# P times v in one piece and w_v split during the second batch, in a fused attention, channel-mix and FFT kernel

## The chip, the cores and the metric

The kernel runs on one core of a Trainium2 chip, in one launch. The core has TensorE (matmul; its weight loads are a row of their own in the profile), VectorE, ScalarE, GpSimd, and the queue of SyncE (SP), which issues most transfers. The metric is the device time in microseconds, the median of several runs; lower is better.

## The reference, cut to what matters

```python
def attention(q, k, v, tau):          # 4 batches, 8 heads, 576 positions, head size 64
    s = q @ k.T / 8
    s = where(s >= s.max(-1) - tau, s, -1e9)
    p = exp(s - s.max(-1)); p /= p.sum(-1) + 1e-9
    return p @ v                       # "P times v"
def channel_mix(x, mu_k, mu_r, w_k, w_v, w_r):     # 512 -> 1024 -> 512
    xp = x shifted by one position
    xk = mu_k*x + (1-mu_k)*xp;  xr = mu_r*x + (1-mu_r)*xp
    return sigmoid(xr @ w_r) * (relu(xk @ w_k)**2 @ w_v)
def last(x, w_ch1, w_ch2):             # 512 -> 2048 -> 512
    u = x + real(fft2(x))
    return u + relu(layernorm(u) @ w_ch1) @ w_ch2
```

The output is last(channel_mix(attention(...))), in fp32.

## The kernel before, in words

Work is written as a Python program whose instructions a planner then orders: it simulates the engines and, for each engine, takes the ready instruction of the highest priority; priority is the order of the program, moved forward by the offset of the high_priority context around it. The table P holds these offsets and the pace of the parts. On the chip each engine works off its list in order.

Attention goes by head pairs: 4 batches x 4 pairs = 16 pairs, each of 9 steps (a step is one 128x576 score tile). ORDER has eight steps of one head (j = 0 or 1) with 128 queries (i = 0 to 3), and in the middle, as step 4, the mixed tile: the 2 x 64 remaining queries of both heads (name em). A step is: scores on TensorE (L218, L232), maximum, threshold and select on VectorE (L258, L273), exponential on ScalarE (L269), scaling by 1/sum on GpSimd (emit_norm, L279). Two steps later (LT) the tile is transposed (emit_T, L318, L326): 512 keys in four 128x128 transposes, and the remainder keys (512 to 575) of both heads in a fifth; ScalarE copies them out to pt (unit) and ptr (rem_unit). The mixed tile was transposed by emit_Tmix, called once for each half of the queries, as its rows belong to both: four transposes (L338) and two matmuls of the remainder keys against 64 rows and 32 columns (L349). P times v is emit_av: for a pair and a half (288 queries), five key blocks x two heads, the heads in the two halves of one PSUM bank, 64 columns of v each as weights (L372; the bank is called avs in batch one and av later). There are 32 such units. They are written by do_av at the steps AC = 7 and 10 after the pair's first.

The first batch (pi < NPAIR) runs attention alone. Beside it all_weights brings w_k (8 pieces of 512 columns), w_r (4) and w_v (7 of 8): a load on SP's queue, three VectorE operations that build fp32 from the raw words (L67 to L69), a copy to a high part (ScalarE, L72) and the subtraction for the low part (GpSimd, L73), in a pool stage1 with two raw buffers; WR pieces are written per step. From step 38 on stage1 is closed, the feed-forward pool (ffn) takes its place, and ffn_stream is drawn on by credits: CN per step, CA at steps with P times v. It computes for each half of a batch w_k (name kps, L392 to L394), w_r (rps, the same lines), w_v (vps, L504 to L506), and the transposes back (xn). The tile t of the gate shares its buffer with the raw words of the eighth piece of w_v, the generator state['late'], whose one load and split run in that pool with one buffer each; the stream finishes it before it writes the gate's matmuls. Pairs of later batches also load raw q and k through one buffer (rawqk, L154) and split them. When attention is over, the rest of the stream runs with the FFT, and then the last part (c1ps, c2ps, L951 to L966).

Of the kernel before, what the change touches and what calls it, by code (L numbers as in the profile page):

```python
# [9 lines left out]
F32 = mybir.dt.float32  # L10
F32R = mybir.dt.float32r
I32 = mybir.dt.int32
ALU = mybir.AluOpType
AF = mybir.ActivationFunctionType
# [4 lines left out]
B, H, S, DH = 4, 8, 576, 64  # L19
D, FF, FC = 512, 1024, 2048  # L20
HS = S // 2
NPAIR = H // 2
P = dict(PRI=100, SR=1.0, CR=2, ORD=0, PF=0, CB=0, XT=0, XL=0, K2=0, FE=0, FE3=0, MU=0, WP=256, C1=2, RB=4, BB=2, FT=4, A0=[7, 8], A1=[11, 12], B0=[7, 8], B1=[11, 12], PT4=1, OR0='', XH=0, SP0=0, CA=1.48, CN=2.22, QS=1, pF=100, pM=100, pN=100, pT=100, pO=100, pE=100, pS=100, pA=0, pX=0, NA=0, LT=2, WS=3, WR=1, CC=3.0, BN=2, OR='FATXOESBI', TM=8, SO=0, SO0=0, AO=0, AO0=0, QS0=0, XD=0, TH=0, SM=0, SM0=0, N0=34, qF=100, qM=100, qN=100, qT=100, qO=100, qE=100, qS=100, qA=100, qX=30, RQ=[0,0,0,0,0,0,0,0], XN=0, QN=36, AVR=0, LX=2, WD=0, WP2=512, E3=1, NA0=0, W0=0, XD2=0, PO=0, WP1=512, IN=[0,1,2,2,4,5,6,7])
P.update({'AC': (7, 10), 'CA': 0.5, 'CN': 2.1, 'pX': 100, 'CR': 3, 'pA': 100, 'OR': 'FTBXOAESI', 'PF': 300, 'pE': 0, 'pO': 500, 'QS': 2, 'WS': 0, 'FE3': 2, 'pF': 0, 'A0': [7, 10], 'C1': 3, 'BN': 2, 'K2': 0, 'WR': 0.6, 'FT': 2, 'MU': 0, 'SR': 0.6, 'XT': 0, 'SO0': 239, 'XL': 3, 'QS0': 2, 'FE': 2, 'CB': 2, 'AO0': 8, 'IN': [0, 0, 2, 2, 5, 6, 6], 'pN': 30, 'pM': 0, 'A1': [10, 13], 'AVR': 1, 'NA0': 170, 'N0': 30, 'PT4': 0, 'WD': 1, 'qN': 0, 'qS': 500, 'qT': 150, 'QN': 37, 'qE': 0, 'qO': 30, 'B0': [7, 10], 'qX': 60, 'qM': 500, 'E3': 1, 'WP1': 512, 'qF': 300, 'OR0': 'FTBXEOASI', 'B1': [10, 13], 'TH': 4, 'AO': 4, 'qA': 30, 'pS': 300, 'SO': 16, 'RQ': [0, 0, 0, 0, 0, 0, 0, 0]})
PRI = P['PRI']


# [1 line left out]
def tile_kernel(ctx: ExitStack, tc: tile.TileContext, a):  # L29
    nc = tc.nc  # L30
    pe, dve, act, pool, sp = nc.tensor, nc.vector, nc.scalar, nc.gpsimd, nc.sync
# [3 lines left out]
    pst = ctx.enter_context(tc.tile_pool(name="pst", bufs=2, space=PSUM))  # L35
# [4 lines left out]
    ident = const.tile([128, 128], F32, name="ident")  # L40
# [37 lines left out]
    def whole(pair, base=0):  # L78
        return lambda c, n: [x[:, c - base:c - base + n] for x in pair]
# [9 lines left out]
    wk = [big(f"A{i}", f"wk{i}") for i in range(2)]  # L89
    wv = [big(f"B{i}", f"wv{i}") for i in range(2)]  # L90
    wr = [wC.tile([128, 2048], F32R, name=f"wr{i}") for i in range(2)]
# [3 lines left out]
    at = astack.enter_context(tc.tile_pool(name="at", bufs=1, side="right"))  # L95
# [40 lines left out]
    NPI = B * NPAIR  # L136
# [100 lines left out]
    def eview(n):  # L237
        pi, tl = step_of(n)
        if tl is None:
            if n not in em:  # L240
                em[n] = at.tile([128, S], F32, tag="em", name="em")
            return em[n]
        j, i = tl
        if (pi, i) not in et:
            m = 4 * pi + i
            if P['E3'] and m % 3 == 2 and m < 4 * NPAIR - 2:
                et[pi, i] = stage.tile([128, 2 * S], F32, tag="e", name="e3")
            else:
                et[pi, i] = at.tile([128, 2 * S], F32, tag="e", bufs=2, name="e")
        return et[pi, i][:, j * S:(j + 1) * S]  # L250
# [25 lines left out]

    def emit_norm(n):
        st, e = stat[n], eview(n)
        pool.tensor_scalar(e, e, st[:, 2:3], 1.0, op0=ALU.mult, op1=ALU.mult)  # L279

    def emit_front(n):
# [14 lines left out]
    def unit(pi, half):  # L296
        if (pi, half) not in ptu:
            ptu[pi, half] = at.tile([128, 2, 4, HS], F32, tag="pt", bufs=3, name="pt")
        return ptu[pi, half]

    def rem_unit(pi, half):
        if (pi, half) not in ptr:
            ptr[pi, half] = at.tile([128, HS], F32, tag="ptr", bufs=2, name="ptr")
        return ptr[pi, half]

    def emit_T(n):
        if not 0 <= n < NSTEP:
            return []
        pi, tl = step_of(n)
        if tl is None:  # L310
            return emit_Tmix(pi, 0)
        j, i = tl
        e = et[pi, i]
        o = 640 if j else 0
        half, sl = i // 2, slice(128 * (i % 2), 128 * (i % 2) + 128)
        t = pst.tile([128, 4, 128], F32, tag="t", name="t")
        for k in range(4):
            pe.transpose(t[:, k, :], e[:, o + 128 * k:o + 128 * (k + 1)], ident)  # L318

        def out():  # L320
            act.activation(unit(pi, half)[:, j, :, sl], t, AF.Copy)  # L321

        todo = [out]
        if j == 1:
            t2 = pst.tile([128, 128], F32, tag="t", name="t2")
            pe.transpose(t2, e[:, 512:640], ident)  # L326

            def out2():
                act.activation(rem_unit(pi, half)[:, sl], t2, AF.Copy)

            todo.append(out2)
        return todo

    def emit_Tmix(pi, half):
        e = em[pi * 9 + 4]
        t = pst.tile([128, 4, 2, 2, 32], F32, tag="t", name="tm")
        for k in range(4):
            pe.transpose(t[:, k].rearrange("p a b c -> p (a b c)"), e[:, 128 * k:128 * (k + 1)], ident)  # L338
        sl = slice(256, HS)

        def out():
            for j in range(2):
                act.activation(unit(pi, half)[:, j, :, sl], t[:, :, j, half, :], AF.Copy)

        def out2():
            t2 = pst.tile([128, 32], F32, tag="t", name="tm2")
            for j in range(2):
                c = 64 * j + 32 * half
                pe.matmul(t2[64 * j:64 * j + 64], e[:, 512:576], ident[:, c:c + 32], start=True, stop=True)  # L349
            act.activation(rem_unit(pi, half)[:, sl], t2, AF.Copy)  # L350

        return [out, out2]

# [11 lines left out]
    def emit_av(pi, half):  # L365

        ps = bank([128, HS], "av")
        v, u, r = vts[pi], ptu[pi, half], ptr[pi, half]
        for k in range(5):
            for j in range(2):  # L370
                w, x = (v[:, 4 * j + k, :], u[:, j, k, :]) if k < 4 else (v[:, 8 + j, :], r)
                pe.matmul(ps[64 * j:64 * j + 64], w, x, start=(k == 0), stop=(k == 4))  # L372

        def post():
            b, pr = divmod(pi, NPAIR)
            x = xunit(pi, half)
            act.activation(x[:, 1:], ps, AF.Copy)
            if half == 1:
                dve.tensor_copy(x[:, 0:1], xT[b, pr, 0][:, HS:HS + 1])
            xdone[half] += 1  # L380

        pending.append(post)


    ffn = {}
# [175 lines left out]
    sstack = ExitStack()  # L561
    stage = sstack.enter_context(tc.tile_pool(name="stage1", bufs=1, side="left"))

    late = 4096 - P['WD'] * P['WP2']

    def all_weights():
        for src, w in (("w_k", wk), ("w_r", wr), ("w_v", wv)):
            yield from weight_pieces(a[src], whole(w), stage, P['WP1'], 0, late if src == "w_v" else None)

    wgen = all_weights()  # L570
    for _ in range(P['W0']):
# [62 lines left out]
    def do_out(n, pi, s):  # L634
        with hp('pO'):
            for f in outs_of.pop(n):
                f()
        do_mix(n, pi, s)

    def do_mix(n, pi, s):  # L640
        if s == P['TM'] and 0 <= pi + (s < 7) * -1 < NPI:
            with hp('pO'):
                for f in emit_Tmix(pi + (s < 7) * -1, 1):
                    f()

    def do_exp(n, pi, s):
        with hp('pE'):
# [12 lines left out]
    def do_X(n, pi, s):  # L660
        if pi < NPAIR:
            if n >= P['WS']:
                state['w'] += P['WR']
                while state['w'] >= 1:
                    state['w'] -= 1
                    next(wgen, None)
        elif state['stream'] is None:
            if n < 9 * NPAIR + 2:
                return
            for _ in wgen:  # L670
                pass
            sstack.close()
            ffn["pool"] = fstackp.enter_context(tc.tile_pool(name="ffn", bufs=1, side="left"))
            state['stream'] = ffn_stream()
            state['late'] = weight_pieces(a["w_v"], whole(wv), ffn["pool"], P['WP2'], late, None, 1, 1, ("t", "xn"))
        elif n < NSTEP:
            with hp('pX'):
                state['credit'] = min(state['credit'] + (P['CA'] if any(s + x in P['AC'] for x in (0, 9)) else P['CN']), P['CC'])
                while state['credit'] > 0:
                    got = next(state['stream'])  # L680
                    if not got:
                        break
                    state['credit'] -= got
                next(state['late'], None)
# [12 lines left out]
    for n in range(NSTEP + 8):  # L697
        pi, s = divmod(n, 9)
# [491 lines left out]
```

## Time and profile before

| | |
|---|---|
| time, median of 3 runs | 1146.96 us (1145.16 to 1150.7) |
| the profiled execution | 1144.78 us, its span 1143.0 us |
| granted TensorE clock, mean | 0.978 |
| busy, share of the span | TensorE 94%, VectorE 60%, ScalarE 45%, GpSimd 36% |

The profile is of one execution. Its time is the device time that the runs report too; the span is from its first to its last instruction. Matmuls are pipelined and their ends are modelled, so the starts of successive matmuls tell more than their durations. av, kps and so on are names of tiles; "x2" in a row is two records.

### The profile page before, as it was taken

Reading aid. Unit: us, or ns where it says so; the run is one execution under the profiler, and the core shown is the slowest. Engines: PE = TensorE matmul, PEld = TensorE weight load, DVE = VectorE, ACT = ScalarE, POOL = GpSimd, SP = SyncE. Lnnn points to the kernel's source line nnn. Section 1 sums busy time; section 2 is a strip of 40 time slices with the busy share of each in tenths; the row PEclk is TensorE's granted clock in tenths of the full one; section 3 lists DMA queues with packets and bytes.
Section 4 is the critical chain, followed back from the end, with each engine's and each line's share of the span. In section 5 each row is a group of like instructions: output and inputs, shape, how many; then the busy total and the mean of one; then the engine's idle time right before and its main releaser. Section 6 shows DMA issues by size and latency. Waiting matters only on the chain.

```text
span 1143.0 us, 19326 instructions
## 1 busy us (share of the span) xinstructions
PE 1072.7 (94%) x7109; PEld 920.4 (81%) x7109; DVE 680.7 (60%) x1765; ACT 519.7 (45%) x1243; POOL 411.9 (36%) x552
## 2 busy tenths in 40 slices
PE   5988689999989989989999987999999999999998
PEld 4655577787877877878789977888989999999997
DVE  6888885555564575576535678975643859323222
ACT  4766666474574674674726644423322222111111
POOL 2434576254363454463523254520010636100000
PEclk9999899999999989999999978999999999999999
DMA  6433311101111120120053245653432546223231
GB/s 234 136 111 116 108 52 49 56 23 55 56 52 31 50 77 13 55 66 13 20 148 106 84 158 181 189 192 117 157 121 101 190 152 189 107 93 105 80 111 56
DMA packets 41429, 114.54 MB, mean 100 GB/s; under 512 B 6207, under 2 KB 6628, under 8 KB 41336
## 3 DMA queue, kind: packets, MB, share of 16 engines
q1 hardware_dynamic: 27920, 74.43, 20.3%
q0 software_dynamic: 10432, 33.50, 9.1%
q10 hardware_dynamic: 2984, 5.38, 1.3%
q8 instruction: 56, 0.92, 0.3%
q14 instruction: 37, 0.30, 0.1%
HBM read 84.98 MB, written 28.32 MB: 99 GB/s over the span
## 4 chain that ended last, share of the span: by engine, by line
PE 76%; DVE 8%; DMA 6%; ACT 5%; issue 3%; POOL 2%; SPq 0%; DVEq 0%; ACTq 0%; POOLq 0%
PE av L372 7%; PE c1ps L951 6%; PE c1ps L953 6%; PE c2ps L964 6%; PE c2ps L966 6%; PE c1ps L952 6%; PE c2ps L965 6%; PE s L218 5%; PE t L318 4%; PE kps L392 3%; PE kps L394 3%; PE kps L393 3%; PE vps L504 2%; PE vps L505 2%; PE vps L506 2%
## 5 line engine op out<-in xcount | busy, mean ns | idle before, releaser
L957 DVE SCALAR_TENSOR_TENSOR hl<-c1ps,hh 128x256 fp32r<-128x256 f32 x144 | 60.6, 422 | 168.5 <-ACT hh L956 167.9
L956 ACT ACTIVATE hh<-c1ps 128x256 fp32r<-128x256 f32 x144 | 54.6, 381 | 224.9 <-PE c1ps L953 224.7
L258 DVE TENSOR_REDUCE small<-s 128x1 f32<-128x576 f32 x144 | 108.1, 753 | 68.5 <-PE s L218 55.4
L273 DVE SCALAR_TENSOR_TENSOR e<-s,small,e 128x576 f32<-128x576 f32 x128 | 102.6, 812 | 56.3 <-ACT e L269 52.8
L279 POOL TENSOR_SCALAR e<-e,small 128x576 f32<-128x576 f32 x112 | 88.6, 796 | 125.9 <-DVE small L610 85.4
L269 ACT ACTIVATE e<-s,small 128x576 f32<-128x576 f32 x128 | 93.4, 745 | 30.3 <-DVE small L258 27.4
L989 POOL DMA_DIRECT2D ud<-u x54 | 29.4, 546 | 202.9 <-DVE u L988 166.6
L318 PE MATMUL t<-ident,e 128*128 128x128 f32 x512 | 86.3, 287 | 9.9 <-POOL e L279 6.3
L321 ACT ACTIVATE pt<-t 128x512 f32<-128x512 f32 x128 | 75.1, 599 | 44.6 <-PE t L318 43.8
L951 PE MATMUL c1ps<-ut,cA 128*128 128x256 f32 x288 | 82.4, 286 | 4.5 <-DVE hl L957 2.5
L318 PEld LDWEIGHTS t<-ident,e 128*128 128x128 f32 x512 | 63.0, 146 | 27.8 <-issue 11.2
L392 PE MATMUL kps<-xh,wk 128*128 128x288 f32 x256 | 78.7, 309 | 3.7 <-ACT xh L418 1.6
L952 PE MATMUL c1ps<-ut,cA 128*128 128x256 f32 x288 | 81.8, 284 | 0.0
L953 PE MATMUL c1ps<-ut,cA 128*128 128x256 f32 x288 | 81.4, 283 | 0.0
L951 PE MATMUL c1ps<-ut,cB 128*128 128x256 f32 x288 | 81.0, 281 | 0.0
L953 PE MATMUL c1ps<-ut,cB 128*128 128x256 f32 x288 | 80.9, 281 | 0.0
L952 PE MATMUL c1ps<-ut,cB 128*128 128x256 f32 x288 | 80.8, 281 | 0.0
L393 PE MATMUL kps<-xl,wk 128*128 128x288 f32 x256 | 76.9, 301 | 1.9 <-POOL xl L420 1.9
L504 PE MATMUL vps<-k,wv 128*128 128x288 f32 x256 | 76.9, 308 | 0.6 <-DVE tg L511 0.6
L394 PE MATMUL kps<-xh,wk 128*128 128x288 f32 x256 | 76.6, 300 | 0.0
L465 POOL TENSOR_TENSOR k<-relu,k 128x288 fp32r<-128x288 f32 x64 | 52.8, 829 | 64.7 <-ACT k L463 50.9
L505 PE MATMUL vps<-k,wv 128*128 128x288 f32 x256 | 75.7, 303 | 0.0
(235 smaller groups left out, 3189.4 us busy)
## 6 DMA issues: line engine op xcount, KB each, us to landing
u<-ud SPq DMA_DIRECT2D x36, 512.0 KB
wraw<-in_w_ch POOLq DMA_DIRECT2D x64, 256.0 KB, 3.2
rawqk<-in_qk SPq DMA_DIRECT2D x24, 608.0 KB
ud<-u POOLq DMA_DIRECT2D x54, 256.0 KB, 2.5
v<-in_v SPq DMA_DIRECT2D x16, 320.0 KB
un<-ud SPq DMA_DIRECT2D x18, 256.0 KB
out<-u SPq DMA_DIRECT2D x18, 256.0 KB
wraw<-in_w_k SPq DMA_DIRECT2D x8, 512.0 KB
```

What stands on the lines that cost most here:

```text
L258: dve.tensor_reduce(st[:, 0:1], sps[n][:, :, 0:HS], axis=AX.XY, op=ALU.max, negate=True)
L269: act.activation(two(eview(n)), sps[n][:, :, 0:HS], AF.Exp, bias=st[:, 0:1])
L273: dve.scalar_tensor_tensor(e, sps[n][:, :, 0:HS], st[:, 1:2], e, op0=ALU.is_ge, op1=ALU.mult, accum_out=st[:, 2:3])
L318: pe.transpose(t[:, k, :], e[:, o + 128 * k:o + 128 * (k + 1)], ident)
L392: pe.matmul(ps, wh, x[0][:, k, :], start=(k == 0), stop=False)
L393: pe.matmul(ps, wh, x[1][:, k, :], start=False, stop=False)
L394: pe.matmul(ps, wl, x[0][:, k, :], start=False, stop=(k == nk - 1))
L504: pe.matmul(ps, wv[0][:, c:c + 128], k2[0][:, k, :], start=(k == 0), stop=False)
L505: pe.matmul(ps, wv[0][:, c:c + 128], k2[1][:, k, :], start=False, stop=False)
L951: pe.matmul(ps, wh, ut[0][:, k, :], start=(k == 0), stop=False)
L952: pe.matmul(ps, wh, ut[1][:, k, :], start=False, stop=False)
L953: pe.matmul(ps, wl, ut[0][:, k, :], start=False, stop=(k == 3))
```

## The change

P times v gets an offset of 1500 (pA, qA) in place of 100 and 30, and takes the remainder keys' block first. The mixed tile is transposed once for both halves: its remainder keys are written twice side by side by an additional GpSimd multiplication, so that a fifth 128x128 transpose puts them on both heads' partitions; two ScalarE copies of twice the columns and two of 64 partitions replace six. ptr holds both halves. w_v leaves the first batch; all its eight pieces are made by the generator late in the feed-forward pool, one per step from step 39 on, and WR goes from 0.6 to 0.4.

```diff
-P.update({... 'pA': 100, ... 'WR': 0.6, ... 'qA': 30, ...})
+P.update({... 'pA': 1500, ... 'WR': 0.4, ... 'qA': 1500, ...})
...
@@ eview
-                em[n] = at.tile([128, S], F32, tag="em", name="em")
-            return em[n]
+                em[n] = at.tile([128, 640], F32, tag="em", name="em")
+            return em[n][:, 0:S]
@@ emit_norm
         st, e = stat[n], eview(n)
+        if n in em:
+            pool.tensor_scalar(em[n][:, S:640], e[:, 512:S], st[:, 2:3], 1.0, op0=ALU.mult, op1=ALU.mult)
         pool.tensor_scalar(e, e, st[:, 2:3], 1.0, op0=ALU.mult, op1=ALU.mult)
@@ rem_unit
-        if (pi, half) not in ptr:
-            ptr[pi, half] = at.tile([128, HS], F32, tag="ptr", bufs=2, name="ptr")
-        return ptr[pi, half]
+        if pi not in ptr:
+            ptr[pi] = at.tile([128, 2, HS], F32, tag="ptr", bufs=2, name="ptr")
+        return ptr[pi][:, half]
@@ emit_T
-            return emit_Tmix(pi, 0)
+            return emit_Tmix(pi)
@@ emit_Tmix
-    def emit_Tmix(pi, half):
+    def emit_Tmix(pi):
...
         sl = slice(256, HS)
+        t2 = pst.tile([128, 128], F32, tag="t", name="tm2")
+        pe.transpose(t2, e[:, 512:640], ident)
 
         def out():
+            for half in range(2):
+                act.activation(
+                    unit(pi, half)[:, :, :, sl], t[:, :, :, half, :].rearrange("p k j c -> p j k c"), AF.Copy
+                )
+
+        def out2():
+            rem_unit(pi, 0)
             for j in range(2):
-                act.activation(unit(pi, half)[:, j, :, sl], t[:, :, j, half, :], AF.Copy)
-
-        def out2():
-            t2 = pst.tile([128, 32], F32, tag="t", name="tm2")
-            for j in range(2):
-                c = 64 * j + 32 * half
-                pe.matmul(t2[64 * j:64 * j + 64], e[:, 512:576], ident[:, c:c + 32], start=True, stop=True)
-            act.activation(rem_unit(pi, half)[:, sl], t2, AF.Copy)
+                p = slice(64 * j, 64 * j + 64)
+                act.activation(
+                    ptr[pi][p, :, sl], t2[p, p].rearrange("p (h c) -> p h c", h=2), AF.Copy
+                )
@@ emit_av
-        v, u, r = vts[pi], ptu[pi, half], ptr[pi, half]
-        for k in range(5):
+        v, u, r = vts[pi], ptu[pi, half], ptr[pi][:, half]
+        for k in (4, 0, 1, 2, 3):
...
-                pe.matmul(ps[64 * j:64 * j + 64], w, x, start=(k == 0), stop=(k == 4))
+                pe.matmul(ps[64 * j:64 * j + 64], w, x, start=(k == 4), stop=(k == 3))
@@ weights of the first batch
-    late = 4096 - P['WD'] * P['WP2']
-
     def all_weights():
-        for src, w in (("w_k", wk), ("w_r", wr), ("w_v", wv)):
-            yield from weight_pieces(a[src], whole(w), stage, P['WP1'], 0, late if src == "w_v" else None)
+        for src, w in (("w_k", wk), ("w_r", wr)):
+            yield from weight_pieces(a[src], whole(w), stage, P['WP1'])
@@ do_out
-        do_mix(n, pi, s)
-
-    def do_mix(n, pi, s):
-        if s == P['TM'] and 0 <= pi + (s < 7) * -1 < NPI:
-            with hp('pO'):
-                for f in emit_Tmix(pi + (s < 7) * -1, 1):
-                    f()
@@ do_X
-            state['late'] = weight_pieces(a["w_v"], whole(wv), ffn["pool"], P['WP2'], late, None, 1, 1, ("t", "xn"))
+            state['late'] = weight_pieces(a["w_v"], whole(wv), ffn["pool"], P['WP2'], 0, None, 1, 1, ("t", "xn"))
```

## Rows read from the trace of the kernel before

**Rows 1.** The page: busy us, share of the span and instructions of each engine.

```profile
PE 1072.7 (94%) x7109; PEld 920.4 (81%) x7109; DVE 680.7 (60%) x1765; ACT 519.7 (45%) x1243; POOL 411.9 (36%) x552
```

**Rows 2.** Windows by stage: busy us (instructions) of each engine, granted clock, DMA share, GB/s.

```profile
0.00:108.00 108.00, 86.92 (x475) 59.03 (x476) 87.63 (x262) 70.25 (x143) 38.60 (x44) 1.00 0.46 148
108.00:165.00 57.00, 42.63 (x255) 33.29 (x255) 49.18 (x131) 35.44 (x77) 35.85 (x39) 0.85 0.29 95
165.00:600.00 435.00, 416.50 (x2936) 348.19 (x2935) 248.82 (x675) 249.09 (x592) 202.94 (x262) 0.98 0.17 51
701.00:1143.00 442.00, 434.29 (x2805) 393.16 (x2805) 227.15 (x527) 107.87 (x279) 91.28 (x149) 0.99 0.40 135
```

**Rows 3.** Waits of TensorE from 165 to 600 us: total us, times, longest us.

```profile
PE s L218 <- DVE e L273: 6.8, 7, 1.5
```

**Rows 4.** TensorE's timeline, a whole unit: start us, us, engine, line, what.

```profile
165.20 2.16 PE L372 MATMUL av<-pt,v 128*64 128x288 f32 x16
...
167.77 0.40 PE L392 MATMUL kps<-xh,wk 128*128 128x288 f32 x1
```

**Rows 5.** TensorE's timeline, a split unit: first row, and where it is over.

```profile
197.85 0.70 PE L372 MATMUL av<-pt,v 128*64 128x288 f32 x2
...
207.34 0.29 PE L505 MATMUL vps<-k,wv 128*128 128x288 f32 x1
207.48 0.30 PE L506 MATMUL vps<-k,wv 128*128 128x288 f32 x1
```

**Rows 6.** Windows, 165 to 600 us, the instructions on av alone.

```profile
165.00:600.00 435.00, 85.94 (x480) 35.25 (x480) 9.94 (x24) 0.98 0.17 51
```

**Rows 7.** TensorE's timeline: half-width matmuls of a mixed tile; four transposes elsewhere.

```profile
307.75 0.30 PE L394 MATMUL kps<-xh,wk 128*128 128x288 f32 x1
307.98 0.31 PE L349 MATMUL tm<-ident,em 128*64 128x32 f32 x4
308.22 0.54 PE L218 MATMUL s<-kh,q 128*128 128x288 f32 x2
...
539.67 0.60 PE L318 MATMUL t<-ident,e 128*128 128x128 f32 x4
540.02 0.38 PE L392 MATMUL kps<-xh,wk 128*128 128x288 f32 x1
```

**Rows 8.** Groups by line, 165 to 600 us, GpSimd: busy us, mean ns, idle before.

```profile
L416 POOL TENSOR_SCALAR xtmp<-xt,small 128x288 f32<-128x288 f32 x48 | 25.2, 534 | 15.1 <-DVE xl L420 7.6 <-ACT xt L377 6.9
```

**Rows 9.** Groups by line, 0 to 165 us, VectorE's part of a weight piece.

```profile
L69 DVE SCALAR_TENSOR_TENSOR wbits<-wraw,wbits 128x512 int32<-128x512 int32 x20 | 15.1, 756 | 0.0
L68 DVE SCALAR_TENSOR_TENSOR wbits<-wraw,wbits 128x512 int32<-128x512 int32 x20 | 14.5, 726 | 0.0
L67 DVE TENSOR_SCALAR wbits<-wraw 128x512 int32<-128x512 int32 x20 | 10.7, 535 | 3.6 <-POOL wv L73 2.6 <-POOL wr L73 0.7 <-POOL wk L73 0.3
```

**Rows 10.** The chain of waits, 125 to 168 us: start us, us, what.

```profile
124.68 0.66 PE av L372 x4
...
141.37 4.84 DMA wraw<-in_w_v
...
151.83 0.64 ACT wv L72
```

**Rows 11.** First and last start, us, of kps and of rps (min/median/max ns).

```profile
L392 PE MATMUL kps<-xh,wk x256: 288/295/406, 147.3 to 658.5; 128*128 128x288 f32 x128
...
L392 PE MATMUL rps<-xh,wr x128: 288/296/607, 181.9 to 682.2; 128*128 128x288 f32 x128
```

**Rows 12.** Waits of SP's queue, 100 to 260 us: total us, times, longest us.

```profile
SPq L154 <- DVE q L187: 108.0, 10, 36.1
```

**Rows 13.** Timelines of GpSimd and VectorE at 136 us.

```profile
136.55 1.41 POOL L164 TENSOR_TENSOR kl<-rawqk,kh 128x576 fp32r<-128x576 f32 x1 [1.52 <-ACT kh L163]
...
136.60 1.91 DVE L69 SCALAR_TENSOR_TENSOR wbits<-wraw,wbits 128x512 int32<-128x512 int32 x1
```

**Rows 14.** TensorE's timeline, a unit in batch one, idle us before it in brackets.

```profile
109.81 4.11 PE L372 MATMUL avs<-pt,v 128*64 128x288 f32 x16 [1.25 <-DVE e L273]
```

More of the change, by code (lines that the diff above doesn't have):

```diff
@@ L23 @@
 P = dict(PRI=100, SR=1.0, CR=2, ORD=0, PF=0, CB=0, XT=0, XL=0, K2=0, FE=0, FE3=0, MU=0, WP=256, C1=2, RB=4, BB=2, FT=4, A0=[7, 8], A1=[11, 12], B0=[7, 8], B1=[11, 12], PT4=1, OR0='', XH=0, SP0=0, CA=1.48, CN=2.22, QS=1, pF=100, pM=100, pN=100, pT=100, pO=100, pE=100, pS=100, pA=0, pX=0, NA=0, LT=2, WS=3, WR=1, CC=3.0, BN=2, OR='FATXOESBI', TM=8, SO=0, SO0=0, AO=0, AO0=0, QS0=0, XD=0, TH=0, SM=0, SM0=0, N0=34, qF=100, qM=100, qN=100, qT=100, qO=100, qE=100, qS=100, qA=100, qX=30, RQ=[0,0,0,0,0,0,0,0], XN=0, QN=36, AVR=0, LX=2, WD=0, WP2=512, E3=1, NA0=0, W0=0, XD2=0, PO=0, WP1=512, IN=[0,1,2,2,4,5,6,7])
-P.update({'AC': (7, 10), 'CA': 0.5, 'CN': 2.1, 'pX': 100, 'CR': 3, 'pA': 100, 'OR': 'FTBXOAESI', 'PF': 300, 'pE': 0, 'pO': 500, 'QS': 2, 'WS': 0, 'FE3': 2, 'pF': 0, 'A0': [7, 10], 'C1': 3, 'BN': 2, 'K2': 0, 'WR': 0.6, 'FT': 2, 'MU': 0, 'SR': 0.6, 'XT': 0, 'SO0': 239, 'XL': 3, 'QS0': 2, 'FE': 2, 'CB': 2, 'AO0': 8, 'IN': [0, 0, 2, 2, 5, 6, 6], 'pN': 30, 'pM': 0, 'A1': [10, 13], 'AVR': 1, 'NA0': 170, 'N0': 30, 'PT4': 0, 'WD': 1, 'qN': 0, 'qS': 500, 'qT': 150, 'QN': 37, 'qE': 0, 'qO': 30, 'B0': [7, 10], 'qX': 60, 'qM': 500, 'E3': 1, 'WP1': 512, 'qF': 300, 'OR0': 'FTBXEOASI', 'B1': [10, 13], 'TH': 4, 'AO': 4, 'qA': 30, 'pS': 300, 'SO': 16, 'RQ': [0, 0, 0, 0, 0, 0, 0, 0]})
+P.update({'AC': (7, 10), 'CA': 0.5, 'CN': 2.1, 'pX': 100, 'CR': 3, 'pA': 1500, 'OR': 'FTBXOAESI', 'PF': 300, 'pE': 0, 'pO': 500, 'QS': 2, 'WS': 0, 'FE3': 2, 'pF': 0, 'A0': [7, 10], 'C1': 3, 'BN': 2, 'K2': 0, 'WR': 0.4, 'FT': 2, 'MU': 0, 'SR': 0.6, 'XT': 0, 'SO0': 239, 'XL': 3, 'QS0': 2, 'FE': 2, 'CB': 2, 'AO0': 8, 'IN': [0, 0, 2, 2, 5, 6, 6], 'pN': 30, 'pM': 0, 'A1': [10, 13], 'AVR': 1, 'NA0': 170, 'N0': 30, 'PT4': 0, 'WD': 1, 'qN': 0, 'qS': 500, 'qT': 150, 'QN': 37, 'qE': 0, 'qO': 30, 'B0': [7, 10], 'qX': 60, 'qM': 500, 'E3': 1, 'WP1': 512, 'qF': 300, 'OR0': 'FTBXEOASI', 'B1': [10, 13], 'TH': 4, 'AO': 4, 'qA': 1500, 'pS': 300, 'SO': 16, 'RQ': [0, 0, 0, 0, 0, 0, 0, 0]})
 PRI = P['PRI']
```

## The prediction

> **What bounds the kernel now.** I read the page's busy line first: TensorE's matmuls cover 94% of the span, the next engine 60% [rows 1]. That alone doesn't say where a saving counts, so I cut the span into stages with the windows view [rows 2]. The reader is to see three regimes. Up to 108 us (batch one, attention alone) TensorE and VectorE are busy about equally long (87 of 108 us), so neither alone sets the pace. From 108 to 165 us, where the feed-forward part comes in, VectorE is busiest (49 of 57 us) and the mean granted clock falls to 0.85. From 165 to 600 us TensorE is busy 416 of 435 us while VectorE, ScalarE and GpSimd stand at 57%, 57% and 47%. The waits of TensorE in that stretch add up to some 18 us over 13 groups; the longest group has 6.8 [rows 3]. So there a microsecond taken from TensorE's own stream is nearly a microsecond of span, and the stream itself has to be read matmul by matmul, in the timeline. After 701 us comes the channel mixing, 434 of 442 us of TensorE, which the change doesn't touch: what is won before it should arrive at the end.
>
> **P times v.** A product is a 64-column matmul that the trace records twice; the two heads of a pair write the two halves of one bank, and ten products (20 records) are a unit. Where a unit is whole, its 20 records run from 165.20 to 167.77 us, 2.57 us to the next matmul, or 0.26 a product [rows 4]. Where it is split, each product stands alone between two matmuls of the feed-forward part: from 197.85 to 207.34 us ten products and ten vps matmuls alternate, 9.49 us [rows 5]. Ten vps would take 10 x 0.14 = 1.4 us by themselves (207.34 to 207.48, same group), the whole unit 2.57, so splitting cost 9.49 - 4.0 = 5.5 us, or 0.61 for each of the nine additional pieces. I counted the pieces in TensorE's timeline: between 165 and 600 us 24 units stand in 70 pieces, 12 of them whole, so there are 46 additional pieces. At 0.6 this is 27.6 us. A second view bears that out: the av matmuls are busy 85.9 us in this stretch [rows 6], against 24 x 2.57 = 62; these 24 and what the neighbours pay make the sum plausible. Before 165 us the count is 18 pieces for 8 units, ten additional, 5 to 6 us.
>
> Why are they split? In the timeline product and vps alternate strictly one to one, which is what a list scheduler does with two chains of equal rank: do_X and do_A both have offset 100. An offset of 1500, when no other exceeds 500, ends the tie. And since the remainder keys' transposes are copied out last, a unit that begins with them begins when all its inputs are there. I take the whole 27.6 as removed from TensorE's stream; the lower bound is 0 (the order stays), the upper the same 27.6, since a unit can't be less than one piece.
>
> **The mixed tile.** Each half now makes four transposes (0.35 us, from 539.67 to 540.02) and two half-width matmuls recorded four times [rows 7]. From the kps matmul before such a pair to the score matmul after it are 0.47 us (307.75 to 308.22), where 0.14 would do: 0.33. Two halves are 2 x (0.35 + 0.33) = 1.36 us; afterwards five transposes, 0.44. That is 0.92 a mixed tile. TensorE's timeline has 22 halves between 165 and 600 us, 11 tiles, so 10 us (bounds 9 and 11, as a tile or half more falls into the stretch). ScalarE makes four copies of it instead of six, the larger two over twice the columns: nothing either way at 57% busy. GpSimd gains a 128x64 multiplication ahead of the mixed tile's; 288 columns take 0.53 [rows 8], so it lies between 0 and 0.53, 16 times, and I take 0.3. It delays the transposes of that tile, which are issued two steps after its scores (a step is about 435/96 = 4.5 us), so it is hidden; without that cover it is 16 x 0.3 = 5 us.
>
> **w_v.** Seven of its eight pieces leave batch one and join the eighth. A piece is three VectorE operations (0.54 + 0.73 + 0.76 = 2.0 us) [rows 9], one on ScalarE and one on GpSimd. In batch one nothing of this is saved before about 97 us, since w_k and w_r stay and the lower pace (0.4 a step) still issues them; of 87 us of VectorE some 4 go before 108 us. TensorE there loses 5 to 6 us of av pieces and 5 x 0.92 of the mixed tile. I take 4 us for the stage, between 0 and 10. In 108 to 165 us two things pull apart. The feed-forward pool can only open when the staging pool is empty, and the chain of waits runs through exactly this: the eighth piece's load, the first thing in the new pool, goes out at 141.37 and takes 4.84 us [rows 10], although the last P times v of batch one ended at 125.3 (first row of that group); kps begins at 147.3 [rows 11]. Staging now empties some 40 us earlier, so up to 16 us of TensorE filler move forward. Against it, eight pieces go through one buffer: the only piece of this kind was issued at 141.37 and had its raw buffer free at 151.8, when ScalarE takes over (the last row of the chain's group), 10.5 us; the least is 4.84 + 2.0 = 6.8. Eight are 55 to 84 us. Their loads need no result of the attention, only the new pool; I put the first at 115, ten before that last P times v, so they end at 170 to 199, and the gate's matmuls (rps) which wait for their tile, began at 181.9 [rows 11]. What stands behind a late piece: on SP's queue the loads of q and k, which already wait there up to 36 us at a time for their buffer [rows 12]; behind the gate's tanh, ScalarE's exponentials. I take a gain of 1, bounds -15 and +16. So the stages before 165 us give 5.
>
> **The sum.** 27.6 + 10 = 38 us go from the 435. Not all stays gone: the same chains of the other engines have to fit into 397 us, and 18 us of waits become longer. Bounds: nothing comes back (the busiest other engine would be at 63%) or all. I choose 12, nearer to nothing because of that 63%: about 6 for waits that grow by a third, and 6 for 24 units that now start the moment their last input lands, 0.25 each. 38 - 12 + 5 = 31. The profiled execution took 1144.8 us (span 1143.0), 2.2 under the median of the runs shown, so 1114 by the profile and 1116 against the median.
>
> **Rivals.** (a) *TensorE stops being the bound*: the shorter stream waits on VectorE and ScalarE and 24 of the 38 us come back. For it: the score matmuls' waits for VectorE [rows 3]. Against: 57% busy. 1128. (b) *The late w_v holds up the gate*. At 84 us it ends at 199, 17 late, and TensorE has attention alone, which in batch one filled it to 80% [rows 2]; if the feed-forward part stands still 17 us and nothing fills it, 1116 + 17 + the 1 taken = 1134. One row makes it worse: a VectorE operation of a piece took 1.91 us, where the mean is 0.76 [rows 9], when it started 0.05 us after a two-input GpSimd operation and ended 0.5 us after it [rows 13]. With 1.2 us lost on each piece it is 10 later, 1144; with 1.2 lost on both two-input operations of each, 8 x 2 x 1.2 = 19, 1153 (0.02 of the chance). Against: the means of 0.73 and 0.76, this one included, leave room for few such cases, though GpSimd was 36% busy in batch one. The Trainium skill's page SBUF — State Buffer, section "SBUF: two separate sides", says that a VectorE operation with two inputs from SBUF and a GpSimd operation exclude each other for a whole instruction, so by that rule moving these to a stage where GpSimd has more to do lengthens them; the trace agrees in that one row. (c) *The order stays split*: only the mixed tile and batch one remain, 10 x 0.7 + 5 = 12, so 1135. (d) *Slower*: remainder first means that TensorE, which issues in order, stops at the head of a unit until the last copy has landed, where before it had nine products to issue. The nearest row: a unit that waited 1.25 us at its head and whose 16 first records were busy 4.11 us [rows 14] instead of 2.16 [rows 4], twice as long, in the stretch where the mean granted clock is 0.85. 1.25 + 1.95 is 3.2 us at worst. The change loses from the point where each of 32 units waits (31 + 6)/32 = 1.2 us; at 2 us it is 1116 - 6 + 64 = 1174. Against: between 165 and 600 us no wait of the twelve whole units is among the longer groups. (e) All 38 us come back: 1142, no change.
>
> **How the numbers follow.** Forecast 0.53, (a) 0.16, (b) 0.12, (c) 0.07, (d) 0.07, (e) 0.05. A measurement of this kernel tells about 0.5% (6 us) from nothing. Forecast, (a), (c) and 0.10 of (b) are faster by more: 0.86; (e) and 0.01 of (b) the same: 0.06; (d) and the rest of (b) slower: 0.08. The forecast's own range is 1100 to 1128. The range for 8 in 10 goes down to 1090 (26 us lower: the 12 not given back and 14 of the 15 that the earlier start could bring over the 1 taken) and up to 1141, past (a), (c) and most of (b); it leaves out (d), (e) and little below.
>
> **What would show it.** In the profile after: av in 32 runs of 20 records of about 2.6 us, av's busy time from 165 to 600 us near 62; no half-width tm matmul; kps starting near 130 us instead of 147; w_v's pieces ending before rps; waits of TensorE in the middle stage not above some 30 us. The prediction is wrong if waits with ScalarE's ptr copy as releaser stand before av (d), if TensorE's idle time in the middle stage grows by tens of us (a), or if a gap opens before the first rps (b).

## The result, and the profile after

The changed kernel takes 1100.15 us (1095.96 to 1103.13, 4 runs) against 1146.06 of the kernel before in the same rounds: a ratio of 0.959, 95% interval 0.954 to 0.964. Forecast were 1116 with a range of 1090 to 1141. The gain is 46 us where the sum had 31.

The page's busy line of the changed kernel answers to [rows 1]: TensorE's matmuls have 54 us less and its weight loads 25; VectorE and ScalarE move by 4 and 2, GpSimd has 9 more.

```profile
PE 1018.6 (93%) x6933; PEld 895.3 (82%) x6933; DVE 684.8 (63%) x1765; ACT 521.4 (48%) x1211; POOL 421.3 (39%) x568
```

For a comparison of equal work the stretches need the same events at their ends. I took the first vps matmul (196 us before, 183 after) and the end of the last P times v (586 and 537). The windows view of the kernel before, cut there (columns as in [rows 2]):

```profile
0.00:196.00 196.00, 159.18 (x945) 117.08 (x946) 154.17 (x440) 127.78 (x275) 95.00 (x108) 0.96 0.37 117
196.00:586.00 390.00, 374.53 (x2630) 311.56 (x2630) 225.42 (x610) 224.15 (x526) 176.89 (x227) 0.98 0.13 42
```

and of the changed kernel, with the channel mixing as its last row:

```profile
0.00:183.00 183.00, 142.31 (x850) 105.50 (x851) 152.71 (x424) 124.02 (x255) 97.25 (x109) 0.97 0.38 123
183.00:537.00 354.00, 336.16 (x2545) 297.92 (x2546) 228.61 (x627) 227.74 (x514) 185.18 (x242) 1.00 0.15 48
...
653.00:1094.00 441.00, 434.51 (x2805) 392.99 (x2805) 227.02 (x524) 109.28 (x279) 89.95 (x148) 0.99 0.40 134
```

The reader is to see that the middle went from 390 to 354 us with TensorE at 96% and 95%, that 13 us were won before it, and that the channel mixing has its 434 us as before, so that what was won before it arrived. TensorE's timeline around a unit, answering to [rows 4, 5]:

```profile
184.86 0.29 PE L513 MATMUL vps<-k,wv 128*128 128x288 f32 x1
185.08 0.71 PE L379 MATMUL av<-ptr,v 128*64 128x288 f32 x4
185.61 2.11 PE L379 MATMUL av<-pt,v 128*64 128x288 f32 x16
187.65 0.53 PE L218 MATMUL s<-kh,q 128*128 128x288 f32 x2
```

From 185.08 to 187.65 are 2.57 us, remainder keys first. All 32 units look like this: 32 pieces of 20 records, where there were 88. The windows view for av alone, over the middle, answers to [rows 6]:

```profile
183.00:537.00 354.00, 57.70 (x438) 29.64 (x440) 8.63 (x21) 1.00 0.15 48
```

It is 57.7 us. TensorE's longest waits in the middle, answering to [rows 3] (total us, times, longest):

```profile
PE s L218 <- DVE e L273: 3.2, 4, 1.3
PE t L328 <- ACT pt L323: 3.1, 4, 1.4
PE xn L529 <- ACT xnat L537: 2.6, 4, 1.0
```

No group of this stretch, the shorter ones included, has ptr's copy as releaser. The first starts of kps and rps, answering to [rows 11]:

```profile
L399 PE MATMUL kps<-xh,wk x256: 288/295/404, 123.6 to 610.2; 128*128 128x288 f32 x128
```

```profile
L399 PE MATMUL rps<-xh,wr x128: 288/295/608, 167.2 to 634.3; 128*128 128x288 f32 x128
```

kps begins 24 us earlier (123.6), rps 15 (167.2). The attention, on the other hand, is two steps behind: 56 maxima had been taken by the first vps instead of 58.

To see what a difference consists of, I added up each trace in one way: over the starts of all matmuls, from the first one until the first of the channel mixing (c1ps), a distance of more than 0.5 us counts as a wait, less 0.25; of what is left, half of the time at a granted clock of 0.50 (the lower level, 1.2 of 2.4 GHz) is "low clock"; the rest is "stream". The half is a convention, near to what the kernel before shows: matmuls of kps, vps and rps start 0.13 us apart at the higher level and 0.24 at the lower (medians). The stretches are those above, and the last runs from the last P times v to c1ps. Times are in us; the ratio is to the kernel before on the same chip.

```
kernel       median   ratio   pieces  to first vps        middle              to c1ps          c1ps at
                              of av   wait  low  stream   wait  low  stream   wait low stream
before       1146.06            88    30.1  7.0  150.7    15.7  5.9  367.8    11.2 5.1  99.2   701.0
changed      1100.15  0.9590    32    35.7  4.5  135.1    18.3  0.0  335.4    11.6 5.2  99.6   653.5
after_again  1101.83  0.9622    32    36.4  7.6  133.7    18.2  1.6  335.0    10.2 6.1  99.5   656.5
av_only      1116.25  0.9754    32    31.2  8.8  146.2    14.7  9.3  338.6    13.1 5.0  99.1   674.6
mix_only     1127.56  0.9844    66    38.2 12.2  142.7    18.6  5.9  345.6    11.9 4.0  99.9   687.3
wv_only      1124.66  0.9825    71    22.8  9.7  141.8    19.7  5.1  358.9    10.2 5.1  99.6   680.9
no_prio      1114.96  0.9742    64    35.7  9.7  143.1    13.7  3.4  341.7    11.4 5.3  99.1   670.9
no_mix       1100.24  0.9612    32    24.3  4.6  138.6    13.4  3.2  347.8    13.3 2.8 100.0   656.5
no_wv        1101.98  0.9631    32    36.3 11.4  140.0    18.5  3.3  329.7    12.2 5.2  99.5   664.3
old_order    1103.94  0.9645    42    31.2  9.7  134.9    20.5  5.0  336.8    12.1 3.9  99.7   662.3
pad_after    1117.25  0.9761    32    29.5  8.4  143.5    14.8  3.3  350.3    11.3 5.2  99.3   674.0
pad_before   1158.58  1.0103   101    22.4  8.0  161.1    11.7  6.5  386.6    10.3 5.6  98.9   718.7
mix_late     1095.09  0.9563    32    23.6  6.9  138.8    20.8  4.9  334.1    11.7 4.4  99.7   653.2
dup_behind   1096.48  0.9572    32    30.5  9.4  133.5    15.7  5.0  333.8    11.4 5.3  99.7   652.5
```

Each line is one profiled execution beside the median of several, and the two can differ: the changed kernel's first profile is of a run 4.2 us under its median, no_wv's of one 3.1 over, pad_before's of one 4.8 over. For the change: stream -47.6, waits +8.6, low clock -8.3, together -47.3 of the 47.5 us by which c1ps moved.

### The profile page after: what moved, and what is told of

Its sections match the earlier page's. It is cut to its first block, busy times and chain, and to the rows that moved or that the text cites. A ratio compares the mean times of both kernels' runs of the same rounds, so it can differ in the third digit from the quotient of the medians.

```text
span 1094.2 us, 18961 instructions
## 1 busy us (share of the span) xinstructions
PE 1018.6 (93%) x6933; PEld 895.3 (82%) x6933; DVE 684.8 (63%) x1765; ACT 521.4 (48%) x1211; POOL 421.3 (39%) x568
## 4 chain that ended last, share of the span: by engine, by line
PE 67%; DVE 9%; DMA 7%; ACT 4%; issue 2%; POOL 2%; DVEq 0%; SPq 0%; ACTq 0%; POOLq 0%
PE c1ps L949 6%; PE c1ps L951 6%; PE c1ps L950 6%; PE c2ps L964 6%; PE c2ps L962 6%; PE c2ps L963 6%; PE av L379 5%; PE s L218 3%; PE t L320 3%; PE kps L399 2%; PE kps L401 2%; PE kps L400 2%; PE vps L511 2%; PE vps L512 2%; PE vps L513 2%
## 5 line engine op out<-in xcount | busy, mean ns | idle before, releaser
L320 PE MATMUL t<-ident,e 128*128 128x128 f32 x512 | 82.2, 276 | 15.7 <-ACT pt L323 5.1
L320 PEld LDWEIGHTS t<-ident,e 128*128 128x128 f32 x512 | 60.7, 141 | 25.8 <-POOL e L281 7.0
L511 PE MATMUL vps<-k,wv 128*128 128x288 f32 x256 | 74.2, 305 | 0.5 <-DVE tg L518 0.5
L512 PE MATMUL vps<-k,wv 128*128 128x288 f32 x256 | 72.1, 299 | 0.0
```

What stands on the lines that cost most here:

```text
L511: pe.matmul(ps, wv[0][:, c:c + 128], k2[0][:, k, :], start=(k == 0), stop=False)
L512: pe.matmul(ps, wv[0][:, c:c + 128], k2[1][:, k, :], start=False, stop=False)
```

## The experiments

**One part at a time.** Theory S: TensorE's stream bounds the middle, and what is taken from it stays gone. Theory W: the surplus over the forecast comes from the earlier feed-forward part.

P times v alone, in the kernel before:

```diff
-'pA': 100, ... 'qA': 30
+'pA': 1500, ... 'qA': 1500
...
-        for k in range(5):
+        for k in (4, 0, 1, 2, 3):
...
-                pe.matmul(..., start=(k == 0), stop=(k == 4))
+                pe.matmul(..., start=(k == 4), stop=(k == 3))
```

> The kernel before with P times v's offset of 1500 and its remainder keys first, nothing else of the change. Theory S (TensorE's stream bounds the middle stage, nothing of what is taken from it comes back): the 46 additional pieces go, 28 us in the middle and some 4 before it, so about 1114. Theory W (the surplus over the forecast comes from the feed-forward part that starts earlier, through w_v): some of the 28 comes back, about 1125. In the profile both expect 32 runs of 20 av records.

1116.25 us, -28.3, 32 pieces; the stream is 34 us shorter and the low clock 5 us more. S had 1114, W 1125.

The mixed tile alone: emit_Tmix, emit_norm, eview and rem_unit of the change in the kernel before, and no second call at step 8.

> The kernel before with the mixed tile transposed once, nothing else of the change. Theory S: 10 us less of TensorE's stream in the middle and up to 4 before, so 1132 to 1136. Theory W: the same work gone but part of it given back, 1138 to 1141.

1127.56, -17.0, more than either theory allowed. The pieces fell too, from 88 to 66, though nothing was done to P times v; I take it that the planner's ties came out otherwise, which no run tests. The stream is 29.5 us shorter, but the waits are 11.7 longer, 8.1 of that before the first vps.

w_v alone, in the kernel before:

```diff
-'WR': 0.6
+'WR': 0.4
...
-        for src, w in (("w_k", wk), ("w_r", wr), ("w_v", wv)):
+        for src, w in (("w_k", wk), ("w_r", wr)):
...
-weight_pieces(a["w_v"], whole(wv), ffn["pool"], P['WP2'], late, None, 1, 1, ("t", "xn"))
+weight_pieces(a["w_v"], whole(wv), ffn["pool"], P['WP2'], 0, None, 1, 1, ("t", "xn"))
```

> The kernel before with all of w_v split in the second batch and the pace of 0.4, nothing else of the change. Theory S: the gate starts some 10 us earlier but the attention falls behind by some steps, so 1136 to 1146. Theory W: this is where the surplus comes from, 1122 to 1132. A late w_v that holds up the gate would show as rps after 182 us and a time above 1146.

1124.66, -19.9: the number of W, but again 17 fewer pieces and 17 us less of stream, which w_v doesn't touch (17 pieces at 0.6 us are 10 of it; the rest is open). So this run doesn't decide for W. The three alone add up to -65, the change has -46.

The offsets taken back from the changed kernel:

```diff
-'pA': 1500, ... 'qA': 1500
+'pA': 100, ... 'qA': 30
```

> The changed kernel with the old offsets of P times v (100 and 30), its remainder keys still first. Theory S: the pieces come back, about 60 of them in the middle, and with them 25 to 30 us: 1125 to 1130. Theory W: 1110 to 1117. If the order of the keys alone kept a unit whole, the time would stay at 1100 and the runs of av at 32.

1114.96, 64 pieces. The time lies in W's range, not in S's: S had expected 1125 or more because it had expected the old number of pieces. But what came back is of the kind that S says: 32 pieces and 14 us of stream, and 15 us of time (13 against after_again). The order of the keys alone doesn't keep a unit whole.

**One part left out, all units whole.** The edits are the two of the first group: no_mix is av_only with w_v's edit, no_wv is av_only with the mixed tile's.

> The changed kernel with the mixed tile transposed once for each half as before. Theory S2 (what each part gained alone was for the most part the same thing, fewer pieces of P times v in the middle stage; with all units whole a part is worth its own work): units whole, 10 to 12 us slower than the changed kernel, 1110 to 1113. Theory W2 (the mixed tile is worth the 17 us that it gained alone): 1117.

1100.24, the same as with the mixed tile's change (0.961 against 0.959 and 0.962). Both theories missed. The table has the reason: against after_again the stream is 18.2 us longer, somewhat more than the 16 x 0.92 = 15 that the mixed tile should be worth, but the waits are 13.8 shorter, 12.1 of them before the first vps, and the low clock is 4.7 less. What the mixed tile gained in the stream, it gave back, most of it in waits.

> The changed kernel with w_v back in the first batch and the pace of 0.6. Theory S2: units whole; w_v's own worth is the earlier start of the feed-forward part less the steps that the attention falls behind, 3 to 8 us, so 1103 to 1108. Theory W2: the 20 us that it gained alone are its own, 1116 to 1120.

1101.98: with whole units w_v's own worth is 2 us or nothing, as the intervals overlap (0.960 to 0.966 against 0.954 to 0.964). W2 is out. That w_v gained 20 alone was for the larger part stream that w_v doesn't touch; that it gained 16 beside av_only (1116.25 to 1100.24) is, by the table, 8 of waits and 12 of low clock, less 2 of stream. The clock isn't the luck of that one pair of profiles: all four runs of av_only were granted 0.972 to 0.974, all four of no_mix 0.978 to 0.985, and (1 - clock) x span, the time that the lower level costs by the same convention, is 31 and 21 us on their means. So some 9 of the 16 go with the clock; why it is higher there, no run shows.

The remainder keys last again, the offset kept:

```diff
-        for k in (4, 0, 1, 2, 3):
+        for k in range(5):
...
-                pe.matmul(..., start=(k == 4), stop=(k == 3))
+                pe.matmul(..., start=(k == 0), stop=(k == 4))
```

> The changed kernel with the remainder keys' block last again, offset 1500 kept. If the offset alone makes the units whole: 32 to 40 pieces and 1098 to 1104. If the order is needed, because a unit begins before its remainder keys are there: over 50 pieces or waits on ptr inside the units, 1106 to 1115.

1103.94, 42 pieces, two more than expected; eight of the ten additional ones stand in batch one, two in the units at 152 and 164 us, none behind them. The offset does nearly all of it. The ratio (0.962 to 0.967) isn't told apart from the changed kernel's.

**Is TensorE the bound?** Redundant work is added to both kernels: the four transposes of every first head's tile are made twice, those of every second head's once.

```diff
-            pe.transpose(t[:, k, :], e[:, o + 128 * k:o + 128 * (k + 1)], ident)
+            for _ in range(2 if j == 0 else 1):
+                pe.transpose(t[:, k, :], e[:, o + 128 * k:o + 128 * (k + 1)], ident)
```

> The changed kernel with the four 128-key transposes of each first head's tile done twice into the same bank (256 additional transposes at 0.09 to 0.11 us, 23 to 28 us of TensorE's stream, three quarters of them in the middle stage; the output is the same). Theory S: TensorE is still the bound there, and 17 to 28 us arrive in the time, 1117 to 1128. Theory A (rival (a): the shorter stream already waits for other engines): below 10 us, 1100 to 1110.

> The kernel before with the same doubled transposes as pad_after (256 more, 23 us of TensorE's stream by that run's profile; the output is the same). Theory S: 17 to 25 us arrive in the time, as in the changed kernel, 1161 to 1170. If TensorE were less of a bound after the change than before, this slope would be clearly above the 17 us of pad_after; if it were clearly below 17, the middle stage of the kernel before had slack that the prediction did not see.

1117.25 (+17.1; 16 to 20 by the ratios to the kernel before on the same chip) and 1158.58 (+12.8 on its own chip, 8 to 16 by its interval). The second is below its range and below the 17 of the first, which by what was expected means slack in the kernel before; the question is where. The middle stretch of each in the windows view, pad_after first:

```profile
190.00:558.00 368.00, 353.32 (x2700) 317.64 (x2701) 225.04 (x623) 227.33 (x512) 184.37 (x241) 0.99 0.14 45
```

```profile
199.00:604.00 405.00, 393.01 (x2786) 330.04 (x2784) 223.86 (x610) 222.10 (x525) 179.97 (x228) 0.98 0.13 40
```

They last 368 and 405 us, against 354 and 390 above: +14 and +15 us, for 14.9 and 18.8 of added stream in the table. Of the first, 3.3 us are low clock, which the changed kernel's first profile has none of. By stream and waits alone 11.4 of 14.9 and 14.8 of 18.8 arrive, 77% and 79% (78% where after_again is the base). So in the middle TensorE is the bound for the most part in both kernels, and as much before as after; rival (a) has nothing for it. The slack is before the first vps, where 10.4 us of added stream moved it by 3.1 in the kernel before (196.1 to 199.2): waits took the rest, 30.1 to 22.4. pad_before isn't work added alone: its units stand in 101 pieces, not 88, and its stream grew by 29 us where pad_after's grew by 23.

**Where the mixed tile's gain went.** TensorE's waits in the changed kernel up to 165 us, the longest groups behind the 8.0 us until the first input:

```profile
PE s L218 <- DVE e L273: 6.7, 9, 1.5
PE tm L340 <- POOL em L281: 4.6, 3, 3.2
PE t L320 <- POOL e L281: 4.1, 3, 1.5
```

The second group isn't among those of no_mix, whose transposes of the mixed tile wait for ScalarE's copies instead (5.8 us in seven waits; here 2.6 in two). One of its three is here, in TensorE's timeline (idle before, and its releaser, in brackets)

```profile
52.50 1.24 PE L218 MATMUL s<-k,q 128*128 128x288 f32 x4 [0.23 <-DVE e L273]
56.92 0.66 PE L340 MATMUL tm<-ident,em 128*128 128x128 f32 x4 [3.18 <-POOL em L281]
```

and this is GpSimd's timeline under it:

```profile
52.61 0.32 POOL L280 TENSOR_SCALAR em<-em,small 128x64 f32<-128x64 f32 x1
53.23 1.11 POOL L173 TENSOR_SCALAR q<-q,small 128x640 f32<-128x640 f32 x1 [0.31 <-DMA q<-in_qk]
54.31 1.40 POOL L164 TENSOR_TENSOR kl<-rawqk,kh 128x576 fp32r<-128x576 f32 x1
55.69 1.18 POOL L281 TENSOR_SCALAR em<-em,small 128x576 f32<-128x576 f32 x1
```

GpSimd makes the additional 64 columns at 52.61, then a pair's q and kl, and scales the mixed tile itself only at 55.69; TensorE stands for 3.18 us. The additional multiplication is 0.32 us of that; the rest is what stands between the two. Two versions follow. Theory G: the waits are the price of doing the tile once in batch one; theory C: they are the luck of a plan. mix_late keeps two calls there:

```diff
-        if n in em:
+        if n in em and n >= 9 * NPAIR:
...
-            return emit_Tmix(pi)
+            return emit_Tmix(pi) if pi >= NPAIR else emit_Thalf(pi, 0)
...
+        if s == P['TM'] and pi < NPAIR:
+            with hp('pO'):
+                for f in emit_Thalf(pi, 1):
+                    f()
```

(emit_Thalf is emit_Tmix of the kernel before), and dup_behind only exchanges two operations:

```diff
-        if n in em:
-            pool.tensor_scalar(em[n][:, S:640], e[:, 512:S], st[:, 2:3], 1.0, op0=ALU.mult, op1=ALU.mult)
         pool.tensor_scalar(e, e, st[:, 2:3], 1.0, op0=ALU.mult, op1=ALU.mult)
+        if n in em:
+            pool.tensor_scalar(em[n][:, S:640], e[:, 512:S], 1.0, 1.0, op0=ALU.mult, op1=ALU.mult)
```

The changed kernel ran again beside them.

> The changed kernel once more, beside the next ones on the same chip: 1097 to 1103. If the low-clock spells of single executions matter, its profile shows another sum of them than the first did, and a span that differs by about half of the difference.

1101.83. Its profile has 5.6 us more of low clock than the first one had, and a span 4.8 longer.

> The changed kernel with the mixed tile transposed once from the second batch on, and once for each half, as before, in batch one. Theory G (done once, it gives its 15 us of stream back in batch one, where TensorE then waits for GpSimd's scaling of the mixed tile and what follows): the stream becomes 4 to 5 us longer, the waits before the first vps about 11 shorter, 1091 to 1096. Theory C (the waits of batch one are the luck of a plan and have nothing to do with the mixed tile): 1100 to 1105.

1095.09, ratio 0.956 (0.954 to 0.959) against after_again's 0.962 (0.960 to 0.964): 6.7 us faster, G's number. The stream before the first vps is 5.1 longer than after_again's and the waits 12.8 shorter, as expected; 4.5 of the 12.8 are the waits for GpSimd's scaling of em (up to 178 us, from the 4.7 of after_again, shown below, to 0.2), the rest is spread over other groups. TensorE's timeline at the same place, where the wait is now 0.25 us:

```profile
51.02 0.28 PE L328 MATMUL t<-ident,e 128*128 128x128 f32 x1
51.54 0.63 PE L365 MATMUL tm<-ident,em 128*128 128x128 f32 x4 [0.25 <-ACT pt L323]
52.01 1.14 PE L218 MATMUL s<-k,q 128*128 128x288 f32 x4
```

The windows view, to be held against the changed kernel's: the first vps comes at 177, not 183.

```profile
0.00:177.00 177.00, 146.76 (x894) 109.55 (x895) 151.76 (x424) 124.21 (x264) 94.10 (x105) 0.95 0.40 127
177.00:537.00 360.00, 339.67 (x2543) 302.22 (x2545) 229.45 (x627) 227.68 (x513) 185.14 (x242) 0.99 0.15 47
```

> The changed kernel with the additional GpSimd multiplication behind the mixed tile's own instead of ahead of it (0.3 to 0.4 us earlier for the first four transposes). If that multiplication is what TensorE waits for in batch one: 1090 to 1096. If not: 1097 to 1103, with the waits on em about as they were.

1096.48, ratio 0.957 (0.955 to 0.959): 5.3 us faster than after_again by an exchange of two lines, and between its two ranges. But the waits on em didn't go. TensorE's, up to 178 us, in after_again and then in dup_behind:

```profile
PE tm L340 <- POOL em L281: 4.7, 4, 2.5
```

```profile
PE tm L343 <- POOL em L281: 4.5, 4, 1.9
...
PE tm L340 <- POOL em L279: 2.9, 3, 1.3
```

The first four transposes (L340) wait for 2.9 us, the fifth (L343), which reads the additional columns, for 4.5: together 7.4, not 4.7. The groups on em in after_again, and then in dup_behind (busy us, mean ns, idle before):

```profile
L281 POOL TENSOR_SCALAR em<-em,small 128x576 f32<-128x576 f32 x16 | 12.8, 800 | 1.1
...
L280 POOL TENSOR_SCALAR em<-em,small 128x64 f32<-128x64 f32 x16 | 6.4, 399 | 21.2 <-DVE small L615 21.2
```

```profile
L279 POOL TENSOR_SCALAR em<-em,small 128x576 f32<-128x576 f32 x16 | 12.0, 750 | 28.3 <-DVE small L615 28.1
...
L281 POOL TENSOR_SCALAR em<-em 128x64 f32<-128x64 f32 x16 | 4.9, 305 | 0.8
```

The multiplications themselves became a little shorter (0.80 to 0.75 and 0.40 to 0.31), 2.3 us in 16 tiles. The waits fell by 5.9 us before the first vps and by 2.5 in the middle, but in other groups: the score matmuls' for VectorE went from 6.5 to 4.1, those of the mixed tile's transposes for ScalarE from 2.6 to none. So the exchange seems to have gained by a plan that came out otherwise, and this run by itself would fit theory C. Part of the gain of both runs is the clock: (1 - clock) x span is 21 us on the mean in mix_late, 22 in dup_behind, 25 in after_again, 22 in the first runs of the changed kernel.

What decides for G is in the table. Three pairs of kernels differ by the mixed tile alone, and with it done once the waits before the first vps are longer each time: before and mix_only (by 8.1 us), av_only and no_wv (5.1), no_mix and the changed kernel (11.4); so too wv_only and no_prio (12.9), which differ by the order of the keys as well. TensorE's waits for GpSimd's scaling of em, up to 178 us, are 3.2 to 5.4 us in these four kernels with it and 0.3 or less in the four without. That this costs time in batch one is shown; why the other groups lengthen with it is not. mix_late is the fastest of all measured, 4.4% under the kernel before. The two weren't tried together.

## Why the prediction was right, point by point

The range held, the sign and the main mechanism were right, and the size was short by 15 of 46 us. Part of that is luck, as two errors cancel in part: the waits in the middle were put 9 us too high, those that the mixed tile brings in batch one at nothing.

**P times v and the tie of offsets: right.** All 46 additional pieces of the middle are gone, and no_prio and old_order show that it was the offset. av_only alone has 29 us less of stream in the middle and 4.5 before it, where 27.6 and 5 to 6 had been read. With the mixed tile, the sum had 38 us of stream in the middle and about 10 before it. Measured: 32.4 and 15.6, 48 in all; that the cut lies at another place, and that two steps of attention moved into the middle, shifts some between the two.

**Rival (d), a wait at the head of each unit: didn't happen.** ptr's copy stands before no unit but for 0.2 us in batch one. The row from which its 3.2 us were taken was read wrong in part: the unit at 109.81 us [rows 14] ran at a granted clock of 0.50, as the windows view shows, so the doubling of its records goes with the clock and not with a wait at the head:

```profile
109.00:115.00 6.00, 5.18 (x21) 2.38 (x22) 5.18 (x16) 2.58 (x5) 3.81 (x4) 0.50 0.53 162
```

**The 12 us given back: the term that was mis-sized.** I chose 12 for waits that grow in the middle; they grew by 2.6 (15.7 to 18.3), and the 24 units that start when their last input lands cost nothing that shows. That is 9 of the 15. TensorE was as much the bound after the change as before it (pad_after, pad_before).

**The mixed tile's multiplication "is hidden": wrong, and with it the mixed tile's gain.** The multiplication was costed at nothing, with 5 us if its cover were gone. The cover was two steps of delay; in batch one the row maxima of successive steps are 2.8 us apart on the mean, not 4.5, and GpSimd's queue has q and kl in it. TensorE waits there for GpSimd's scaling of em in every kernel that does the tile once, and the waits before the first vps are 5 to 13 us longer. They grew by 5.6 in the first profile of the changed kernel. So the mixed tile, counted at 10 us in the middle and 4.6 before it, is about right in the stream (16 to 18 us against no_mix) and brought nothing in time beside the other two parts (no_mix); kept out of batch one, it is worth some 5 us, if anything (mix_late 0.954 to 0.959, no_mix 0.958 to 0.964: the intervals just meet). What the additional multiplication costs by itself is open, as dup_behind's gain doesn't lie in the waits on em.

**w_v and rival (b): the gate wasn't held up.** The changed kernel's SP queue loads its first piece at 92.70 us, not 115:

```profile
92.70 0.33 SPq L54 DMA_DIRECT2D wraw<-in_w_v  x1
...
130.78 14.08 SPq L54 DMA_DIRECT2D wraw<-in_w_v  x3
```

The chain of waits shows the seventh's load and its last VectorE operation:

```profile
136.80 3.54 DMA wraw<-in_w_v
...
142.97 1.53 DVE wbits L69
```

Eight pieces at some 7.5 us each, between the 6.8 and the 10.5 of the bounds, end before 156, and rps starts at 167.2. The third operation of a piece did lengthen where GpSimd has more to do, from 0.76 [rows 9] to 0.91 on the mean (groups by line, 88 to 165 us). It is what rival (b) spoke of, but on three of the eight pieces: those at 129.57, 135.66 and 142.97 us began while a GpSimd operation was running and took 1.18, 1.12 and 1.53 us; the other five took 0.67 to 0.71. That is 0.15 us a piece instead of 1.2. The group, and the longest of the three in the timeline:

```profile
L69 DVE SCALAR_TENSOR_TENSOR wbits<-wraw,wbits 128x512 int32<-128x512 int32 x8 | 7.3, 908 | 0.0
```

```profile
142.54 1.41 POOL L164 TENSOR_TENSOR kl<-rawqk,kh 128x576 fp32r<-128x576 f32 x1
...
142.97 1.53 DVE L69 SCALAR_TENSOR_TENSOR wbits<-wraw,wbits 128x512 int32<-128x512 int32 x1
```

kps started at 123.6 where I had looked for 130, and the first vps came 13 us earlier with the attention two steps behind. The stages before 165 us were put at 5; whether that was too little can't be read from the 13, as two steps' work moved into the middle. In time, w_v is worth 2 us or nothing beside the other two parts (no_wv).

**The low clock: not in the sum.** 8.3 us less of it in the profile of the changed kernel, 2.7 in that of after_again (18.0 against 15.3). Over all runs it is less than in the first profile: (1 - clock) x span is 26 us on the mean of the kernel before's 21 runs of the experiments and 23.5 on that of the changed kernel's eight, 2 to 3 us apart. The rest is the luck of the execution that was profiled, the fastest of its four.

Taken together, by the second profile of the changed kernel, which is nearer to the median: c1ps came 44.5 us earlier, 49.5 of stream and 2.7 of low clock less 7.8 of waits. The sum had 48 of stream, of which it let 17 go (the 12, and 5 of the 10 before the middle). So of what the forecast lacks some 9 us are waits that didn't grow, 2 to 3 the clock and 1 to 2 the stream; what is left to the 15 is within the scatter of the runs.

## What to carry to other kernels

Where one engine is the bound over a whole stage, count how often its stream changes its kind of work: two chains of equal priority that alternate cost more than either's instructions show, and an offset that ends the tie can be worth more than work taken out. Ablate in both directions: three parts that each gain alone can gain the same thing, and only the runs with one part left out show what each is worth beside the others. A delay is not hidden because it is short on the average: look at the stage where the cover is thinnest, and apply the edit only where it pays, as mix_late does. And an exchange of two lines can gain through the plan alone: whether it gained where it was meant to, the waits tell and the time doesn't.

## What the runs showed of the hardware that I hadn't expected

The granted clock differs between executions of the same program: means of 0.985 and 0.979 in the two profiles of the changed kernel, with spans of 1094.2 and 1099.0 us. In the kernel before three spells at the lower level stood in the middle stage; TensorE had waited before the first of them, as the windows view shows (1.3 of 3 us busy at clock 1.00, then fully busy at 0.52):

```profile
259.00:262.00 3.00, 1.31 (x13) 1.03 (x12) 2.94 (x7) 3.00 (x8) 2.96 (x3) 1.00 0.00 0
262.50:266.00 3.50, 3.50 (x18) 3.47 (x18) 2.31 (x10) 1.01 (x2) 1.78 (x3) 0.52 0.63 212
```

The changed kernel's first profile has waits of 1.3 and 1.4 us in that stage too (above) and no spell at all, the second profile one. I had not expected either that the price of an interleaved 64-column piece would arrive as time nearly whole: with 56 pieces fewer, av_only has 34 us less of stream and is 28 us faster.
